# Attention's output rows stored for two tiles at a time, with their buffers first in SBUF

## The chip, the cores and the metric

The kernel runs on one core of one Trainium2 chip. The metric is the device time of one execution in microseconds (us); the time before is the median of three runs.

## The reference

Three layers follow each other. Decayed causal attention without a softmax runs over 8 sequences, 8 heads, 576 positions and 64 features per head. Its result, read as 4608 tokens of 512 features, goes through a mixture of 8 experts in which each token takes only its best expert. The result goes through a third, dense layer with a squared ReLU.

```python
scores = scale * np.matmul(q, k.transpose(0, 1, 3, 2))
ret = scores * Dmat[None, :, :, :]
x = np.matmul(ret, v)            # tokens x 512
...
expert_idx = np.argmax(x @ w_gate, axis=1)
out[mask] = gate_w[mask, None] * (np.maximum(x[mask] @ w1[e], 0.0) @ w2[e])
...
g = np.maximum(x @ w_in, 0.0) ** 2
return g @ w_out
```

## The kernel before

Attention works on 36 tiles of 128 tokens, in a loop over `t` (line 636). Four tiles and a half make one sequence: of every nine tiles, eight belong to one sequence each, four after four, and the ninth holds the last 64 positions of both. `kind(t)` gives a tile's sequence and its place `c` in it (0 to 3, and 4 for the ninth).

A round of the loop does the following, in this order.

- `load(t + 4)` (lines 357 to 364) fetches the inputs of the tile four rounds ahead from `att` in one DMA of 1 MB (768 KB for a ninth tile). There are five buffers of them (`in_p`), so the load waits until the engines have finished with tile t-1.
- In some early rounds small tables are fetched (`tabx`, `idn`, `cf`, `sel`, lines 640 to 651).
- The list `late` of the round before is worked off: four DMAs (line 456) that store the rows of tile t-1, 64 KB each, into the DRAM buffer `x_d`, and for some tiles a store of the logits (`l_d`, line 494).
- In rounds 12, 18, 24 and 30 `load_unit` (line 107) fetches 512 KB of the first experts' weights (`raw`).
- `scores(t + 1)` multiplies keys and queries on TensorE (line 387, `sc`), and VectorE masks them (line 393, `r`).
- `scale_v(t + 2)` scales the values on GpSimd (line 374, `vs`).
- In every second round the transposes of `fold()` (line 476) and the matmuls of `logits()` (line 467) run on TensorE for two tiles at a time.
- `out_x(t)` (lines 420 to 460) sums the tile's output in PSUM (lines 428, 435 and 439). VectorE scales it into `x` (line 447), half of a buffer for two tiles, and transposes it in blocks of 32 into `xr` (line 449), a buffer of 2 KB per partition. There are three such buffers (`xr_p`, one tile each). The round then puts the store of `xr` on the list `late`.
- `state(t)` updates the running state (line 411, `stp`), which ScalarE copies out (line 418, `sts`).
- One step of the routing of a group of finished tiles is taken from the list `todo`.

All these DMAs are issued by the SP queue, in the order of the program. Each of them signals one of eight semaphores (`DMAHW0` to `DMAHW7`), which are used in turn; before an issue the queue waits until the earlier DMA on the same semaphore has landed.

In round 31 `lead_rows` (line 582) fetches the first 256 routed rows from `x_d` with two indirect DMAs of GpSimd (line 270, `lead`); in rounds 33 and 34 TensorE transposes them (line 286, `turn`), and after the loop it starts on the first expert with them. The other rows of the first expert are gathered from `x_d` when the last group is routed (`gather(0, ...)`, `xs<-x_d,gidx`), and their transposed halves go into `xt` (line 782).

The pools of the attention part are opened one behind the other from the left of SBUF: tables, a weight buffer, the five input buffers, `vs`, `r`, and last `xr_p`. When they are closed the pools of the expert stage take the same bytes: `xt_p` first, then `w_b`, then `h_p`, the hidden layer. A new tile waits for what used its bytes before.

Behind attention come the experts (lines 794 to 832) and the dense layer (from line 1106); the change doesn't touch them.

Of the kernel before, what the change touches and what calls it, by code (L numbers as in the profile page):

```python
# [7 lines left out]
F32 = mybir.dt.float32  # L8
# [41 lines left out]
def body(ctx, tc, att, tab_v, tab_x, masks, wg, ident, pick, cst, wu, wd, out):  # L50
# [3 lines left out]
    def scope(stack, name, bufs, space=None, side=None, reuse=None):  # L54
        kw = {"space": space, "side": side, "reuse_waits": reuse}
        kw = {k: v for k, v in kw.items() if v is not None}
        return stack.enter_context(tc.tile_pool(name=name, bufs=bufs, **kw))
# [14 lines left out]
    x_d = dram.tile([NTOK, 512], F32, name="x_d")  # L72
# [253 lines left out]
    lg_ps = scope(chain, "lg_ps", 1, PSUM, side="right")  # L326
    rt_ps = scope(chain, "rt_ps", 1, PSUM, side="right")
    with ExitStack() as es:
        tabs = scope(es, "tabs", 1)
        pools["stg"] = scope(es, "astg", 1)  # L330
        in_p = scope(es, "in_p", 5)
        sp_p = scope(es, "sp_p", 3)
        r_p = scope(es, "r_p", 2)
        xr_p = scope(es, "xr_p", 3)
        sc_ps = scope(es, "sc_ps", 3, PSUM)
        x_ps = scope(es, "x_ps", 2, PSUM)
        st_ps = scope(es, "st_ps", 1, PSUM)
# [6 lines left out]
        zq = tabs.tile([128, 4, 3, 64], F32, name="zq")  # L344
        sts = [tabs.tile([128, 4, 128], F32, name=f"sts{i}") for i in range(4)]

        in_t, vs_t, r_t, st_acc, xp_t = {}, {}, {}, {}, {}
        lead_s = []
        late = []

        def kind(t):
            g, c = divmod(t, 9)
            if c == 8:
                return None, 4
            return 2 * g + c // 4, c % 4
# [42 lines left out]
        def stslot(b, c):  # L398
            return sts[2 + b % 2] if c == 3 else sts[c % 2]
# [20 lines left out]
        def out_x(t):  # L420
            b, c = kind(t)
            q = in_t[t][:, 0].rearrange("p (h n) -> p h n", h=4)
            ps = x_ps.tile([128, 4, 128], F32, tag="x", name="x")
            if c == 4:
                for i in range(2):
                    s = stslot(i, 3)
                    for p in range(4):
                        pe.matmul(
                            ps[:, p], s[:, p], zq[:, p, i:i + 2].rearrange("p a n -> p (a n)"),
                            start=(p == 0 and i == 0), stop=False, skip_group_check=True,  # L430
                        )
            elif c > 0:
                s = stslot(b, c - 1)
                for p in range(4):
                    pe.matmul(ps[:, p], s[:, p], q[:, p], start=(p == 0), stop=False, skip_group_check=True)
            for p in range(4):
                for s in range(2):
                    h = 2 * p + s
                    pe.matmul(
                        ps[64 * s:64 * s + 64, p], vs_t[t][:, 64 * h:64 * h + 64],  # L440
                        r_t[t, s][:, p],
                        start=(c == 0 and p == 0), stop=(p == 3), skip_group_check=True,
                    )
            if t % 2 == 0:
                xp_t[t // 2] = xp_p.tile([128, 4, 256], F32, tag="x", name="x")
            x = xp_t[t // 2][:, :, 128 * (t % 2):128 * (t % 2) + 128]
            vec.tensor_tensor(out=x, in0=ps, in1=tabx[:, c], op=ALU.mult)
            xr = xr_p.tile([128, 4, 4, 32], F32, tag="xr", name="xr")
            vec.transpose(
                out=xr.rearrange("q t k j -> q k t j"), in_=x.rearrange("q k (t i) -> q k t i", i=32)  # L450
            )

            def put():
                rows = x_d[128 * t:128 * t + 128, :].rearrange("(t i) (a c) -> a i t c", i=32, a=4)
                for a in range(4):
                    sp.dma_start(
                        out=rows[a], in_=xr[32 * a:32 * a + 32].rearrange("q t k j -> q t (k j)")
                    )

            late.append(put)  # L460

        def logits(j):
# [173 lines left out]
        for t in range(NT):  # L636
# [3 lines left out]
            if t in (1, 2, 4):  # L640
                c = {1: 2, 2: 3, 4: 4}[t]
# [18 lines left out]
            if fold:  # L660
                fold()
                for g in GROUPS:
                    if g[1] == t - 2:
                        todo += group(*g)
            fold = logits((t - 3) // 2) if t % 2 and t > 2 else None
            out_x(t)
            state(t)
            if t + 1 < NT:
# [82 lines left out]
    with ExitStack() as es:  # L751
# [259 lines left out]
        for u in range(NU):  # L1011
# [4 lines left out]
            if u + 1 in work:  # L1016
                what, j, r = work[u + 1]
# [11 lines left out]
            if u in work:  # L1029
                what, j, r = work[u]  # L1030
# [75 lines left out]
    with ExitStack() as es:  # L1106
# [217 lines left out]
        def tile_of(T, what, a, b):  # L1324
            return first_of[T] + ((7 * a + KEPT.index(b)) // 4 if what == "up" else 14 + 8 * a + b // 2)
# [49 lines left out]
        for m, (T, what, a, b) in enumerate(slots):  # L1375
# [23 lines left out]
            t = tile_of(T, what, a, b)  # L1399
# [85 lines left out]
```

## Time and profile before

| | us |
|---|---|
| median of three runs (1402.28, 1406.72, 1415.77) | 1406.72 |
| profiled execution | 1416.54 |
| its span on the core | 1414.7 |
| TensorE busy in the span | 1359.7 (96%) |
| VectorE, ScalarE, GpSimd busy | 831.8, 547.0, 375.4 |

The profiled execution lasted 1.8 us more than the span of its instructions. A busy share is an average over stages that have different limits; the attention loop is the first eighth of the span. In the views below PE is TensorE, PEld its weight loads, DVE VectorE, ACT ScalarE, POOL GpSimd, and SPq the SP queue that issues DMAs. L456 is line 456 of the kernel before. A share of the DMA engines is the mean over sixteen of them.

### The profile page before, as it was taken

To read this page: it belongs to the slowest core of one execution; us is meant where nothing else is said; L and a number is where in the kernel's file an instruction comes from. 1 tells how busy PE (TensorE), PEld (TensorE's weight loads), DVE (VectorE), ACT (ScalarE), POOL (GpSimd) and SP (SyncE) were. 2 spreads that over 40 slices of the span, in tenths; PEclk is the share of its full clock that TensorE was granted. 3 is DMA by queue.
4 is the path that set the end of the run, shared out by engine and by line. 5 is a ranking of instruction groups with operands and counts; after the bars stand their busy time and mean duration, and the time that the engine had idled before them with its cause. 6 is when DMAs were issued, how large, how long until landed. Compare 5 with 4: busy or idle time off the path is not lost.

```text
span 1414.7 us, 21636 instructions
## 1 busy us (share of the span) xinstructions
PE 1359.7 (96%) x8121; PEld 1161.9 (82%) x8121; DVE 831.8 (59%) x1512; ACT 547.0 (39%) x1064; POOL 375.4 (27%) x408
## 2 busy tenths in 40 slices
PE   8988898999989999899999999999999999999998
PEld 6877787888878889798988888888888888888887
DVE  5666765686967768673785466245742556334422
ACT  1222233453434445342554444244432444234321
POOL 2223345747456474611231013000210003000000
PEclk9999999999999999999999999999999999999999
DMA  9999844666666675656776666567666666665563
GB/s 318 291 287 290 249 137 153 219 217 210 210 197 193 199 246 186 208 173 251 275 272 224 212 233 225 205 208 229 222 234 212 214 207 230 212 234 183 204 212 115
DMA packets 107713, 311.03 MB, mean 220 GB/s; under 512 B 20430, under 2 KB 55758, under 8 KB 85584
## 3 DMA queue, kind: packets, MB, share of 16 engines
q1 hardware_dynamic: 97728, 288.41, 59.9%
q0 software_dynamic: 9872, 21.15, 5.1%
q8 instruction: 66, 1.08, 0.3%
q14 instruction: 47, 0.39, 0.1%
HBM read 257.98 MB, written 52.58 MB: 220 GB/s over the span
## 4 chain that ended last, share of the span: by engine, by line
PE 77%; DMA 10%; issue 6%; POOL 2%; DVE 2%; ACT 1%; another core or an unknown queue 1%; SPq 1%; POOLq 0%; DVEq 0%; ACTq 0%
PE b L1149 23%; PE fa L1223 9%; PE fa L1221 9%; PE fa L1222 9%; DMA in<-att 5%; PE l L808 4%; PE acc L830 4%; PE l L807 4%; PE l L806 4%; PE acc L831 4%; PE acc L832 4%; DMA raw<-wu 1%; POOL xs L270 1%; DMA x_d<-xr 1%
## 5 line engine op out<-in xcount | busy, mean ns | idle before, releaser
L1149 PE MATMUL b<-xt,wq 128*128 128x512 f32 (+1 forms) x1296 | 264.7, 362 | 1.8 <-ACT xt L743 0.7
L1149 PEld LDWEIGHTS b<-xt,wq 128*128 128x128 f32 x1296 | 220.9, 188 | 40.6 <-ACT xt L743 1.1
L1221 PE MATMUL fa<-wq,ch 128*128 128x512 f32 x576 | 224.3, 389 | 0.0
L1223 PE MATMUL fa<-wq,cl 128*128 128x512 f32 x576 | 224.3, 389 | 0.0
L1222 PE MATMUL fa<-wq,ch 128*128 128x512 f32 x576 | 224.3, 389 | 0.0
L1211 DVE TENSOR_TENSOR cl<-g,ch 128x512 fp32r<-128x512 f32 (+1 forms) x160 | 108.9, 689 | 173.7 <-ACT ch L1210 171.2
L734 POOL TENSOR_TENSOR xsum<-yf 128x256 f32<-128x256 f32 x80 | 64.1, 809 | 452.3 <-DVE yf L722 386.9
L270 POOL DMA_INDIRECT xs<-x_d,qidx x140 | 154.9, 1106 | 40.0 <-issue 34.9
L1210 ACT ACTIVATE ch<-g 128x512 fp32r<-128x512 f32 (+1 forms) x160 | 91.5, 584 | 182.4 <-PE fa L1222 181.4
L806 PE MATMUL l<-xt,w 128*128 128x320 f32 (+1 forms) x480 | 150.5, 314 | 6.7 <-issue 5.0
L808 PE MATMUL l<-xt,w 128*128 128x320 f32 (+1 forms) x480 | 150.6, 314 | 5.1 <-issue 5.0
L807 PE MATMUL l<-xt,w 128*128 128x320 f32 (+1 forms) x480 | 150.7, 314 | 4.3 <-issue 4.2
L831 PE MATMUL acc<-w,hh 128*128 128x512 f32 x320 | 128.5, 402 | 3.0 <-issue 3.0
L830 PE MATMUL acc<-w,hh 128*128 128x512 f32 x320 | 129.1, 403 | 2.2 <-issue 1.8
L832 PE MATMUL acc<-w,hl 128*128 128x512 f32 x320 | 127.9, 400 | 2.4 <-issue 2.4
L1223 PEld LDWEIGHTS fa<-wq,cl 128*128 128x128 f32 x576 | 108.1, 188 | 22.5 <-DVE cl L1211 0.2
L1222 PEld LDWEIGHTS fa<-wq,ch 128*128 128x128 f32 x576 | 108.2, 188 | 22.5
L1221 PEld LDWEIGHTS fa<-wq,ch 128*128 128x128 f32 x576 | 108.1, 188 | 22.3
L812 ACT ACTIVATE hh<-l 128x320 fp32r<-128x320 f32 (+2 forms) x128 | 54.6, 436 | 178.4 <-PE l L808 107.3
L1135 ACT ACTIVATE s<-b 128x512 f32<-128x512 f32 (+1 forms) x120 | 66.5, 555 | 104.8 <-PE b L1149 104.6
L813 DVE SCALAR_TENSOR_TENSOR hl<-l,hh 128x320 fp32r<-128x320 f32 (+2 forms) x128 | 59.3, 485 | 79.7 <-ACT hh L812 54.0
L806 PEld LDWEIGHTS l<-xt,w 128*128 128x128 f32 x480 | 90.9, 189 | 9.5 <-issue 4.8
(182 smaller groups left out, 2113.0 us busy)
## 6 DMA issues: line engine op xcount, KB each, us to landing
wq<-ws_d SPq DMA_DIRECT2D x142, 1024.0 KB
raw<-wu SPq DMA_DIRECT2D x62, 512.0 KB
in<-att SPq DMA_DIRECT2D x28, 1024.0 KB
craw<-wd SPq DMA_DIRECT2D x32, 512.0 KB
ws_d<-cw SPq DMA_DIRECT2D x24, 512.0 KB
x_d<-xr SPq DMA_DIRECT2D x144, 64.0 KB
out<-fo SPq DMA_DIRECT2D x32, 256.0 KB
yq<-y_d SPq DMA_DIRECT2D x112, 64.0 KB
```

Of the source, the lines that this page charges most:

```text
L270: pool.indirect_dma_start(out=xs, out_offset=None, in_=src, in_offset=bass.IndirectOffsetOnAxis(ap=index, axis=0),)
L806: pe.matmul(ps, w[:, 0, k], hi[:, k, cs], start=(k == 0), stop=False)
L807: pe.matmul(ps, w[:, 0, k], lo[:, k, cs], start=False, stop=False)
L808: pe.matmul(ps, w[:, 1, k], hi[:, k, cs], start=False, stop=(k == 3))
L830: pe.matmul(acc[i], hh[:, cs], w[:, 0], start=(f == 0), stop=False)
L831: pe.matmul(acc[i], hh[:, cs], w[:, 1], start=False, stop=False)
L832: pe.matmul(acc[i], hl[:, cs], w[:, 0], start=False, stop=(f == 7))
L1149: pe.matmul(ps, w[:, a, c], xc[T][i, b][c], start=(i in (5, 1, 4) and m == 0), stop=(m == 5), skip_group_check=True,)
L1211: vec.tensor_tensor(out=lo[:, o], in0=s, in1=hi[:, o].bitcast(F32), op=ALU.subtract)
L1221: pe.matmul(acc[i], hi[:, cs], w[:, 0], start=(f == 0), stop=False)
L1222: pe.matmul(acc[i], hi[:, cs], w[:, 1], start=False, stop=False)
L1223: pe.matmul(acc[i], lo[:, cs], w[:, 0], start=False, stop=(f == 15))
```

## The change

The transposed rows of two tiles now share one buffer of 4 KB per partition, and there are three of those. The tile with even `t` takes a new one, transposes into its first half and stores nothing; the tile with odd `t` transposes into the second half and puts four stores of 128 KB on the list `late`, each for the rows of both tiles. A row in `x_d` is still written in pieces of 512 bytes. The pool `xr_p` is opened first of attention's pools, so that its 12 KB per partition lie where the tables lay, and all others move up.

```diff
     with ExitStack() as es:
+        xr_p = scope(es, "xr_p", 3)
         tabs = scope(es, "tabs", 1)
...
         r_p = scope(es, "r_p", 2)
-        xr_p = scope(es, "xr_p", 3)
...
-        in_t, vs_t, r_t, st_acc, xp_t = {}, {}, {}, {}, {}
+        in_t, vs_t, r_t, st_acc, xp_t, xr_t = {}, {}, {}, {}, {}, {}
...
-            xr = xr_p.tile([128, 4, 4, 32], F32, tag="xr", name="xr")
+            if t % 2 == 0:
+                xr_t[t // 2] = xr_p.tile([128, 8, 4, 32], F32, tag="xr", name="xr")
+            xr = xr_t[t // 2]
             vec.transpose(
-                out=xr.rearrange("q t k j -> q k t j"), in_=x.rearrange("q k (t i) -> q k t i", i=32)
+                out=xr[:, 4 * (t % 2):4 * (t % 2) + 4].rearrange("q t k j -> q k t j"),
+                in_=x.rearrange("q k (t i) -> q k t i", i=32),
             )
+            if t % 2 == 0:
+                return
 
             def put():
-                rows = x_d[128 * t:128 * t + 128, :].rearrange("(t i) (a c) -> a i t c", i=32, a=4)
+                rows = x_d[128 * t - 128:128 * t + 128, :].rearrange("(t i) (a c) -> a i t c", i=32, a=4)
                 for a in range(4):
                     sp.dma_start(
                         out=rows[a], in_=xr[32 * a:32 * a + 32].rearrange("q t k j -> q t (k j)")
```

The SP queue issues 645 rows instead of 717 (a row is an instruction, and a loop of the expert stage counts once). In rounds 14 to 16 of the attention loop it held, before, a load (`in<-att`) and the four stores of the tile before (`x_d<-xr`) in each round; the names in brackets are what each waits for, the DMA semaphores and the engines:

```order
L364 DMA in<-att 128x2048 [waits DMAHW1_49,PE_49,Pool_49]
L456 DMA x_d<-xr 32x4x128 [waits DMAHW2_49,DVE_49]
L456 DMA x_d<-xr 32x4x128 [waits DMAHW3_49]
L456 DMA x_d<-xr 32x4x128 [waits DMAHW4_49]
L456 DMA x_d<-xr 32x4x128 [waits DMAHW5_49]
L364 DMA in<-att 128x2048 [waits DMAHW6_49,PE_49,Pool_49]
L456 DMA x_d<-xr 32x4x128 [waits DMAHW7_49,DVE_49]
L456 DMA x_d<-xr 32x4x128 [waits DMAHW0_49]
L456 DMA x_d<-xr 32x4x128 [waits DMAHW1_49]
L456 DMA x_d<-xr 32x4x128 [waits DMAHW2_49]
L364 DMA in<-att 128x2048 [waits DMAHW3_49,PE_49,Pool_49]
```

The third store of the second round waits for semaphore 1, which is that of the first load above. On the same queue in the same rounds, 14 to 16, the changed kernel has:

```order
L364 DMA in<-att 128x2048 [waits DMAHW5_49,PE_49,Pool_49]
L461 DMA x_d<-xr 32x8x128 [waits DMAHW6_49,DVE_49]
L461 DMA x_d<-xr 32x8x128 [waits DMAHW7_49]
L461 DMA x_d<-xr 32x8x128 [waits DMAHW0_49]
L461 DMA x_d<-xr 32x8x128 [waits DMAHW1_49]
L364 DMA in<-att 128x2048 [waits DMAHW2_49,PE_49,Pool_49]
L364 DMA in<-att 128x2048 [waits DMAHW3_49,PE_49,Pool_49]
L461 DMA x_d<-xr 32x8x128 [waits DMAHW4_49,DVE_49]
L461 DMA x_d<-xr 32x8x128 [waits DMAHW5_49]
L461 DMA x_d<-xr 32x8x128 [waits DMAHW6_49]
L461 DMA x_d<-xr 32x8x128 [waits DMAHW7_49]
```

Two loads now follow each other, and the stores of two tiles come in one block behind them. The second store of round 16 waits for semaphore 5, that of the load of round 14, and the first for semaphore 4, that of the load of round 13.

At the start of the loop, in rounds 1 and 2, the SP queue held before the load of tile 5, a table, the four stores of tile 0, and then the load of tile 6:

```order
L364 DMA in<-att 128x2048 [waits DMAHW7_49,PE_49,Pool_49]
L642 DMA tabx<-tab_x 128x512 [waits DMAHW0_49]
L456 DMA x_d<-xr 32x4x128 [waits DMAHW1_49,DVE_49]
L456 DMA x_d<-xr 32x4x128 [waits DMAHW2_49]
L456 DMA x_d<-xr 32x4x128 [waits DMAHW3_49]
L456 DMA x_d<-xr 32x4x128 [waits DMAHW4_49]
L364 DMA in<-att 128x2048 [waits DMAHW5_49,PE_49,Pool_49]
L642 DMA tabx<-tab_x 128x512 [waits DMAHW6_49]
L646 DMA idn<-ident 128x128 [waits DMAHW7_49]
```

The same rounds of the changed kernel's SP queue:

```order
L364 DMA in<-att 128x2048 [waits DMAHW7_49,PE_49,Pool_49]
L647 DMA tabx<-tab_x 128x512 [waits DMAHW0_49]
L364 DMA in<-att 128x2048 [waits DMAHW1_49,PE_49,Pool_49]
L647 DMA tabx<-tab_x 128x512 [waits DMAHW2_49]
L651 DMA idn<-ident 128x128 [waits DMAHW3_49]
L461 DMA x_d<-xr 32x8x128 [waits DMAHW4_49,DVE_49]
L461 DMA x_d<-xr 32x8x128 [waits DMAHW5_49]
L461 DMA x_d<-xr 32x8x128 [waits DMAHW6_49]
L461 DMA x_d<-xr 32x8x128 [waits DMAHW7_49]
```

The load of tile 6 and two tables moved ahead of the first stores, which are now those of tiles 0 and 1. On the other engines the instructions stand as before.

## Rows read from the trace of the kernel before

**Rows 1.** The page: TensorE and DMA in 40 slices; packets by size.
```profile
PE   8988898999989999899999999999999999999998
...
DMA  9999844666666675656776666567666666665563
...
DMA packets 107713, 311.03 MB, mean 220 GB/s; under 512 B 20430, under 2 KB 55758, under 8 KB 85584
```

**Rows 2.** Chain of waits, 84 to 110 us: start, length, what.
```profile
79.74 8.90 DMA x_d<-xr
...
88.71 8.17 DMA in<-att
...
98.11 8.06 DMA in<-att
...
108.61 8.71 DMA in<-att
```

**Rows 3.** Timeline of the SP queue, 93 to 112.4 us: start, issue time, what.
```profile
93.28 0.58 SPq L364 DMA_DIRECT2D in<-att  x1
...
98.11 0.39 SPq L364 DMA_DIRECT2D in<-att  x1
...
101.50 0.30 SPq L456 DMA_DIRECT2D x_d<-xr  x1
...
101.84 0.43 SPq L456 DMA_DIRECT2D x_d<-xr  x1
102.32 0.57 SPq L107 DMA_DIRECT2D raw<-wu  x1
103.00 0.58 SPq L364 DMA_DIRECT2D in<-att  x1
...
106.19 0.33 SPq L456 DMA_DIRECT2D x_d<-xr  x1
...
112.08 0.31 SPq L456 DMA_DIRECT2D x_d<-xr  x1
```

**Rows 4.** Waits of the SP queue, 45 to 160 us.
```profile
SPq L456 <- DMA in<-att: 38.3, 25, 2.6
```

**Rows 5.** Instructions on the input tiles, 45 to 160 us: durations, first and last start.
```profile
L364 SPq DMA_DIRECT2D in<-att x24: 351/471/1576, 46.4 to 155.3; - x24
```

**Rows 6.** Busy time by stretch; the last two columns are DMA share and GB/s.
```profile
10.00:25.00 15.00, 13.55 (x194) 11.95 (x194) 6.79 (x11) 2.65 (x7) 4.92 (x5) 0.94 1.03 392
25.00:30.00 5.00, 3.10 (x44) 2.37 (x40) 3.22 (x6) 0.76 (x2) 1.34 (x2) 0.90 0.78 215
45.00:160.00 115.00, 98.17 (x1461) 84.03 (x1459) 77.43 (x165) 26.57 (x65) 32.86 (x28) 0.99 0.93 289
176.00:179.30 3.30, 3.30 (x37) 3.01 (x36) 3.13 (x10) 0.00 (x0) 0.00 (x0) 1.00 0.37 89
```

**Rows 7.** Waits of VectorE, 45 to 160 us.
```profile
DVE xr L449 <- DMA x_d<-xr: 24.7, 20, 2.8
DVE x L447 <- PE x L439: 12.5, 11, 2.4
```

**Rows 8.** Timeline of the SP queue, 13 to 22 us.
```profile
14.01 5.11 SPq L456 DMA_DIRECT2D x_d<-xr  x4
21.60 0.35 SPq L364 DMA_DIRECT2D in<-att  x1
```

**Rows 9.** Chain of waits, 158 to 172 us, and TensorE's timeline there.
```profile
161.50 6.96 DMA lead<-x_d,lead_idx
...
168.51 0.66 PE L286 MATMUL turn<-idn,lead 128*128 128x128 f32 x4 [0.47 <-DMA lead<-x_d,lead_idx]
```

**Rows 10.** Timelines of the SP queue and of GpSimd behind the loop.
```profile
180.02 1.77 SPq L456 DMA_DIRECT2D x_d<-xr  x4
...
189.34 1.00 POOL L270 DMA_INDIRECT xs<-x_d,gidx  x1 [18.87 <-DVE g L266]
```

**Rows 11.** Chain of waits, 119.1 to 131.5 us.
```profile
123.23 1.09 PE sc L387 x16
...
130.84 0.49 PE stp L411 x16
```

## Prediction

> **What bounds the kernel now.** I read the page's forty slices first [rows 1]. TensorE is at 8 tenths or more in every slice, so over the whole span it is the bound; the DMA engines stand at 9 tenths in the first four slices alone, about 140 us, and those are the attention loop that the change touches. There the next view is the chain of work [rows 2]: from 88.71 to 117.3 us it is almost only loads of attention's inputs, 8.06 to 8.71 us each, with short pieces of the SP queue between them. TensorE shows up on the chain for longer runs only later. The stage is therefore bound by its loads, and what the change is worth is read from what a load waits for.
>
> The SP queue tells that [rows 3]. Each DMA on it signals one of eight semaphores in turn, and waits first until the DMA that used the same one eight places earlier has landed (both listings of the change show the waits). A tile now has one load and four stores, so the third store of a tile always waits for the load issued at the start of the round before. In [rows 3] the load issued at 93.28 us lands and lets a third store go at 101.50, and the one of 98.11 does so at 106.19; the next load stands behind that store. In the stretch from 45 to 160 us this wait is 38.3 us in 25 times [rows 4], one for each tile. So two loads are in flight at most, and one for the moment between a landing and the next issue. Two rounds last one load and what stands behind its landing: in [rows 2] the load of 88.71 lands after 8.17 us, and the next but one is issued at 98.11, 9.40 us later, or 4.70 per tile. The loop's own count agrees: 24 issues from 46.4 to 155.3 us [rows 5], 108.9 / 23 = 4.74 us per tile.
>
> Is a load's 8 us latency, or are the DMA engines full? [rows 6] has three stretches. While almost only loads run (10 to 25 us) they move 392 GB/s at a share of 1.03. While stores alone run (176 to 179.3) 89 GB/s take a share of 0.37: 1.22 us of the sixteen engines for 294 KB. In the mixed stretch they are at 0.93, but with only 289 GB/s. A tile's load, 1.05 MB at 392 GB/s, is 2.68 us; its stores, 262 KB at 1.22 us for 294 KB, are 1.09; the 23 rounds, 7 to 29, also hold three weight loads of 0.52 MB (rounds 12, 18 and 24), which add 3 x 1.34 / 23 = 0.17. That makes 3.94 of the 4.74 us. The remaining 0.80 us per tile is lost: 0.33 as idle engines (0.07 x 4.74), and 0.47 as packets that last longer than in either pure stretch. It isn't a tax on every byte: between the landings at 106.19 and 112.08 [rows 3] one more load of 0.52 MB was fetched (issued at 102.32, directly before another load), and that interval, 5.89 us, is only 1.20 longer than the 4.69 before it, at 437 GB/s for the added bytes. A load behind a load is cheap; what costs is the change from stores to a load, one per tile.
>
> **The change part by part.** Stores: 144 of 64 KB become 72 of 128 KB. The bytes and the rows of 512 bytes stay, so the 1.09 us of the engines per tile stay. The queue's order becomes load, four stores, load, load, four stores: one change from stores to a load in two tiles instead of two. If the lost 0.80 us belongs to these changes, half of it goes: 0.40 us per tile. Its ends: nothing, if it belongs to bytes that are mixed; and 0.47 / 2 + 0.33 = 0.57, if the idle part goes as well. I take 0.40, since the row of 112.08 puts it on the change of direction, and since some idleness is bound to stay. It counts for the loads of tiles 6 to 35: 30 x 0.40 = 12.0 us, with ends 0 and 17.
>
> Semaphores: with six DMAs for two tiles, the waits that fall on loads are now on the first two stores of a pair. The load of tile t+3 stands behind the landing of tile t's, three stores and itself (about 1.9 us by the issue times in [rows 3]); three rounds must hold 8.17 + 1.9 us, so this queue no longer binds above 3.4 us per tile. SP's own time falls as well; it is no bound either way.
>
> The transposes: the buffer of a tile is now free when its store of three tiles before has landed. In 45 to 160 us VectorE waits 24.7 us for that, 20 times [rows 7]. A store can take 8.90 us to land [rows 2]. Three buffers of two tiles each give four rounds between a pair's issue and the next write into its buffer, some 17 us, so this wait goes. I count nothing for it: VectorE's next wait in [rows 7] is TensorE, and TensorE's in this stage is the load. Were that cover gone, it is inside the 0.80 us.
>
> The start: the load of tile 6 is issued at 21.60 us, after the first tile's four stores, which take SP from 14.01 to 19.1 [rows 8]; now it stands ahead of them. The engines have a share of 0.78 from 25 to 30 us [rows 6], so at most 1.1 us is gained, and none is lost; I take 1.0.
>
> What is late next: the first routed rows are fetched at 161.50 us and reach TensorE 6.96 us later, two rounds after their indices [rows 9]; TensorE then waits 0.47 us for them. Two rounds shorter by 0.80 us together leave 0.8 us uncovered: I take 0.8 off, ends 0 and 2. At the end the last stores go out together with those of the tile before, 256 KB more, 1.1 us at the rate above. The gather that needs them starts at 189.34 us [rows 10], 7.5 us after the last store's issue at about 181.8, and it waits for VectorE's indices: nothing, and at most 1.1 if that cover were gone.
>
> The pool's place: the row buffers lie under the two buffers that the first expert's columns take, where before they lay under the hidden layer's last ones. Those columns are written after the gather, which needs all stores anyway; nothing, and at most the same 1.1 us.
>
> Sum: 12.0 + 1.0 - 0.8 = 12.2 us. The profiled execution took 1416.54 us (span 1414.7, 1.8 around it), 0.7% over the median of the runs shown, 1406.72; it becomes 1404.3 us, and the median 1394.5.
>
> Here the Trainium skill speaks against the change. Its page "DMA: Bandwidth & Descriptors", section "Why small descriptors are slow", puts the price of small transfers on the single descriptor (a fixed overhead in each, and metadata for each), and a store's rows remain 512 bytes on both sides. By that rule alone the stores would cost what they cost, and the gain would be nothing, the second rival below. The page of the profile agrees that most packets are small: 55758 of 107713 are under 2 KB [rows 1]; but 437 GB/s for a load behind a load is not in that rule, and so it doesn't decide.
>
> **The rivals.** TensorE's own pace: from 123.23 to 131.33 us the chain is TensorE without a gap [rows 11], two tiles in 8.10 us, 4.05 per tile. If the whole lost time goes, the loop falls to this floor: 30 x (4.74 - 4.05) = 20.7 us, 1386.0. For it: the sum of the pure rates, 3.94 us, is below the floor. Against: with two bounds this close, each waits for the other at times.
>
> Nothing happens: the lost 0.80 us goes with stores beside loads, however they are grouped, and the loop stays at 4.74. The time is 1406 give or take 3. For it: the bytes, rows and buffers of loads are unchanged. Against: the 437 GB/s.
>
> Slower: in the SP queue two loads now stand behind four stores whose first two wait for the two loads before, so loads are issued in bursts. This decides when three rounds of 4.74 us no longer hold a load and the 1.9 us behind it: from 12.3 us of a load's latency. To be 14.1 us slower, 1%, it takes 0.47 us more per tile, a latency of 13.7; that gives 1421. Latency is 8.06 to 8.71 us, and a burst of stores twice as long adds 1.09, so there is room. If transposes still waited for stores, the change wouldn't do what it says: by [rows 7] and 8.90 us to land against 17 there is no case for it.
>
> **How the numbers follow.** One per cent, 14.1 us, is about what a measurement of this kernel tells from no change. The forecast, 1394.5 us, has a chance of 0.55, with a range of its own from 1388 to 1401; some 45% of it lies below 1392.6. TensorE's floor has 0.19, nothing 0.18, slower 0.08. Faster by over 1%: 0.55 x 0.45 + 0.19 = 0.44. Slower by over 1%: 0.08. Within 1%: 0.48. The range reaches from a little under the floor to the case of nothing: 1384 to 1407.
>
> **What would show it.** Right: the x_d stores appear 72 times; the wait of the transposes for them is gone; loads in the stretch come every 4.2 to 4.4 us with a DMA rate above 305 GB/s; the first transposed tile of the first expert comes 10 to 14 us earlier, and everything behind is shifted by as much. Wrong: still 4.7 us per tile with the transposes free (then the lost time belongs to mixed bytes), a pace of 4.05 with TensorE gapless (then the switch cost all of it), load latencies over 12 us (then the bursts), or a gain in the loop that is gone by the end.

## The result and the profile after

The changed kernel takes 1386.05 us in the median of five runs (1383.41 to 1394.09). Its time is 0.9858 of the time before, with a 95% interval from 0.9808 to 0.9907: 20.0 us less, 13.1 to 27.0. The profiled execution took 1389.07 us with a span of 1387.3. It is 27.5 us shorter than the profiled one of before, which lay 9.8 us over its median while this one lies 3.0 over its own; the medians differ by 20.7. Ratios are formed from undisturbed runs alone, so they can differ a little from the quotient of two medians.

The page first, against [rows 1]: TensorE, DMA engines and packets.

```profile
PE   8999998998999989999999999999999999999998
...
DMA  9999644566757656665866676656666766565563
...
DMA packets 106560, 311.02 MB, mean 224 GB/s; under 512 B 19278, under 2 KB 54606, under 8 KB 84432
```

1153 packets are gone, and TensorE's row has a 9 in four of its first five slices, where it had one. The stretches that answer to [rows 6], with the engines' columns first and the clock, DMA share and GB/s last:

```profile
25.00:30.00 5.00, 4.31 (x72) 3.65 (x68) 4.47 (x8) 1.17 (x4) 1.04 (x1) 1.00 1.06 390
45.00:160.00 115.00, 113.57 (x1687) 97.97 (x1686) 96.12 (x200) 31.38 (x75) 38.22 (x31) 1.00 0.92 308
45.00:140.00 95.00, 93.99 (x1432) 81.22 (x1431) 80.39 (x162) 25.09 (x61) 31.62 (x26) 1.00 1.01 346
```

From 45 to 160 us TensorE is busy for 113.57 us instead of 98.17. The third row ends soon after the last load's issue at 136.3 us: 346 GB/s, where [rows 6] had 289. The attention loop is now bound by TensorE, as the chain of waits says for 84 to 112 us (start, length, what), where [rows 2] had loads of 8 us:

```profile
85.12 1.09 PE sc L387 x16
...
89.68 1.09 PE sc L387 x16
...
95.22 1.23 DVE a L227
...
99.77 1.60 DVE b L240
...
101.86 1.31 PE sc L387 x16
...
106.32 1.09 PE sc L387 x16
...
110.16 1.09 PE sc L387 x16
```

Between these stand other matmuls and, from 93.10 to 101.42 us, a piece of VectorE's work (routing, masks, scaling and transposes); no load. The waits of the SP queue, 45 to 160 us, against [rows 4]:

```profile
SPq L364 <- PE stp L411: 26.2, 11, 4.4
SPq L461 <- DVE xr L451: 13.4, 8, 5.7
```

The 38.3 us of waiting for loads to land are gone, all but 1.1: the loads now wait until TensorE has finished with a buffer, and the stores until VectorE has written the rows. The loads themselves (against [rows 5]):

```profile
L364 SPq DMA_DIRECT2D in<-att x23: 328/454/2131, 45.4 to 136.3; - x23
```

That is 90.9 / 22 = 4.13 us per load instead of 4.74. A loop's pace is better read from what it produces. The transposes between 45 and 145 us, first in the kernel before:

```profile
L449 DVE STREAM_TRANSPOSE xr<-x x21: 711/711/714, 45.9 to 141.5; 128x512 f32<-128x512 f32 x21
```

and after:

```profile
L451 DVE STREAM_TRANSPOSE xr<-x x25: 711/711/714, 47.0 to 142.6; 128x512 f32<-128x512 f32 x25
```

95.6 us held 20 tiles before and 24 after, 4.78 and 3.98 us per tile. VectorE waits for no store any more; what is left against [rows 7] is TensorE:

```profile
DVE x L447 <- PE x L439: 13.8, 14, 2.3
```

Behind the loop (timelines of GpSimd and TensorE, against [rows 9, 10]), the first expert's gather starts at 167.50 us instead of 189.34, 21.8 us earlier, and the transposes of the lead rows start with no wait in front:

```profile
140.50 1.19 POOL L270 DMA_INDIRECT lead<-x_d,lead_idx  x1 [3.52 <-DVE lead_idx L592]
...
167.50 1.00 POOL L270 DMA_INDIRECT xs<-x_d,gidx  x1 [18.79 <-DMA raw<-wu]
```
```profile
146.81 0.66 PE L286 MATMUL turn<-idn,lead 128*128 128x128 f32 x4
```

### The profile page after: what moved, and what is told of

Same layout as the page of the kernel before. It is cut to its first block, busy times and chain, and to the rows that moved or that the text cites. A ratio compares the mean times of both kernels' runs of the same rounds, so it can differ in the third digit from the quotient of the medians.

```text
span 1387.3 us, 21515 instructions
## 1 busy us (share of the span) xinstructions
PE 1352.8 (98%) x8121; PEld 1159.2 (84%) x8121; DVE 835.3 (60%) x1512; ACT 547.3 (39%) x1064; POOL 377.3 (27%) x408
## 3 DMA queue, kind: packets, MB, share of 16 engines
q8 instruction: 66, 1.08, 0.3%
## 4 chain that ended last, share of the span: by engine, by line
PE 83%; issue 6%; DMA 4%; DVE 3%; POOL 2%; ACT 1%; another core or an unknown queue 1%; SPq 0%; DVEq 0%; POOLq 0%; ACTq 0%
PE b L1154 24%; PE fa L1227 9%; PE fa L1228 9%; PE fa L1226 9%; PE l L811 4%; PE l L813 4%; PE l L812 4%; PE acc L835 4%; PE acc L836 4%; PE acc L837 3%; PE sc L387 2%; PE x L439 2%; PE x L435 1%; POOL xs L270 1%
```

## The experiments

Four theories were open, of which the prediction held the first. **A**: each change from stores to a load costs, and there are half as many. **B**: the transposes no longer wait for stores. **C**: with fewer DMAs per tile the eight semaphores come round more slowly, so more loads are in flight. **D**: the place of the pool matters.

### e1: the buffers alone

```diff
+        xr_p = scope(es, "xr_p", 6)
...
-        xr_p = scope(es, "xr_p", 3)
```

This is the kernel before, with six buffers of one tile and the pool first.

> The kernel before with six buffers for the transposed rows of one tile each (pool first) instead of three: the transposes no longer wait for stores, while loads and stores keep their order, sizes and number. If the changes from stores to a load are what cost (theory A), or the eight semaphores (theory C): the loop stays at 4.6 to 4.8 us per tile and the time within 4 us of before. If the gain came from freeing the transposes (theory B): 4.0 us per tile and about 20 us less than before, as in the changed kernel.

Measured: 1408.3 us (1396.66 to 1420.16), 0.9972 of before [0.9933, 1.001]. Its SP queue waits, 45 to 160 us, and its transposes over the whole program:

```profile
SPq L456 <- DMA in<-att: 38.9, 24, 2.5
```
```profile
L449 DVE STREAM_TRANSPOSE xr<-x x36: 711/711/714, 11.5 to 177.7; 128x512 f32<-128x512 f32 x36
```

Its profiled execution, 1420.16 us, is the longest of its ten runs, so only its loop is read here. The transposes have no wait for stores, and yet the loop from the first to the last lasts 166.2 us; in the kernel before it is 166.1:

```profile
L449 DVE STREAM_TRANSPOSE xr<-x x36: 710/711/714, 13.2 to 179.3; 128x512 f32<-128x512 f32 x36
```

The queue's wait for loads is what it was. B falls, and so does the pool's place as a gain by itself.

### e2: two pair stores in every round

```diff
-                for a in range(4):
...
+                def some(these):
+                    for a in these:
...
+                some((0, 1))
+                late.append(lambda: some((2, 3)))
```

The changed kernel, with the same 72 stores of 128 KB, but two of them in each round: load, two stores, load, two stores. There is a change from stores to a load in every tile again.

> The changed kernel with the four 128 KB stores of a pair issued two in the even and two in the odd round: as few DMAs and semaphores, the same buffers, but again one change from stores to a load in each tile. Theory A: most of the gain is lost, 4.4 to 4.7 us per tile and 12 to 20 us more than the changed kernel. Theories B (transposes) and C (semaphores): as the changed kernel, 4.0 us per tile, within 4 us of it.

Measured: 1387.36 us (1383.05 to 1389.78), 0.9859 [0.981, 0.9909]: as the changed kernel.

```profile
L451 DVE STREAM_TRANSPOSE xr<-x x36: 711/711/714, 13.1 to 157.0; 128x512 f32<-128x512 f32 x36
```

The loop lasts 143.9 us; that of the changed kernel, 11.5 to 157.4, lasts 145.9. A change of direction in every tile costs this loop nothing, and A falls. A price that TensorE's pace could hide is looked for in m3 below.

### e3: pairs in eight stores of 64 KB

```diff
-                for a in range(4):
+                for h in range(2):
+                    for a in range(4):
```

The changed kernel with the grouping of two loads and one block of stores, but each store halved.

> The changed kernel with each pair stored in eight DMAs of 64 KB at once instead of four of 128 KB: changes from stores to a load as in the changed kernel, but ten DMAs for two tiles on the eight semaphores, as before. Theory A alone: 4.0 to 4.2 us per tile, within 6 us of the changed kernel. Theory C: the eighth store waits for the load issued just ahead of the block, so that at most two loads are in flight: 4.5 us per tile or more, 12 to 25 us more than the changed kernel. Theory B: as the changed kernel.

Measured: 1418.41 us (1411.77 to 1426.15), 1.0078 [1.0047, 1.0108], slower than before. The SP queue's waits, 45 to 140 us, and the transposes:

```profile
SPq L462 <- DMA in<-att: 31.2, 18, 3.1
```
```profile
L451 DVE STREAM_TRANSPOSE xr<-x x36: 711/711/715, 11.6 to 183.7; 128x512 f32<-128x512 f32 x36
```

With ten DMAs for two tiles the seventh and eighth store take the semaphores of the two loads directly ahead of the block. The queue stands until these have landed, and only then come the next loads. The loop lasts 172.1 us, and the time is 32.4 us over the changed kernel's, more than the 12 to 25 expected for C. This speaks for C, but a fixed price for each DMA of 64 KB would do the same; the next six kernels take that apart.

### m1 to m4: the transfers alone

These kernels compute nothing of the reference. They only move attention's bytes: 36 loads of 1 MB into five buffers, and 9.4 MB of stores. For every one or two tiles the loop issues (written short):

```diff
-        load(t); store(t, 1)                                           # m1
+        load(t); load(t + 1); store(t, 2)                              # m2
+        load(t); store(t, 2, (0, 1)); load(t + 1); store(t, 2, (2, 3)) # m3
+        load(t) for all t; then store(t, 2) for all pairs              # m4
```

`store(t, 1)` is four stores of 64 KB, `store(t, 2)` four of 128 KB for two tiles, and with two numbers in brackets only two of these.

> Attention's DMAs alone, without any computation: 36 loads of 1 MB into five buffers and 144 stores of 64 KB, in the order of before (one load, four stores). Theory A, with pure rates of 2.68 us for a load and 1.09 for a tile's stores and about 0.8 us for a change from stores to a load: 4.5 us per tile, 155 to 170 us. If a change of direction costs nothing: 3.8 us per tile, 135 to 140 us.

> The same bytes in the order of the changed kernel: two loads, four stores of 128 KB. Theory A: half the changes, 4.1 us per tile, 10 to 20 us less than with one load and four stores. If the cost belongs to mixed bytes or there is none: the same time as that run within 4 us.

> The same 128 KB stores, but two behind each load. Theory A: as with one load and four stores of 64 KB, 4.4 us per tile or more, although there are as few DMAs as in the order of pairs. If the number of DMAs is what counts (theory C): as the order of pairs.

> All 36 loads first, then all 72 stores of 128 KB: one change of direction. Every theory: the sum of the pure rates, 36 x 3.77 = 136 us or a little less, 2.6 to 2.7 us for a load and 1.0 to 1.1 for a tile's stores. It gives the floor against which the other three orders are held.

Measured, one execution each: m1 172.72 us, m2 123.94, m3 125.96, m4 131.43. Two met neither of their numbers: m1 is slower than both, and m2 is 48.8 us below it, where A had 10 to 20. So m1 has the pace of the loop before, 4.6 to 4.75 us per tile, with no engine computing at all. m3 changes direction in every tile and takes 2.0 us more than m2, 0.11 us for each of 18 further changes if they are all of it, while m4, with one change in all, is slower than both. A falls a second time. The loads of m1 in 20 to 100 us, and how long one takes from issue to landing:

```profile
L48 SPq DMA_DIRECT2D in<-att x17: 430/569/767, 23.2 to 96.6; - x17
...
DMA to landing us min/median/max: 7.8/8.1/8.6
```

and of m3:

```profile
L48 SPq DMA_DIRECT2D in<-att x24: 398/428/471, 22.7 to 97.1; - x24
...
DMA to landing us min/median/max: 9.1/9.2/9.8
```

In m3 a load takes longer to land, 9.2 instead of 8.1 us, and yet they come every 3.23 us (74.4 / 23) instead of 4.59 (73.4 / 16): three are in flight instead of two. With five DMAs per tile the third store waits for the load of the round before, and one more store and the next load stand behind it, so two rounds hold a load's time to land and these three issues: (8.1 + 2 x 0.45 + 0.57) / 2 = 4.8 us per tile, with 0.45 us for a store's issue and 0.57 for a load's. With three DMAs per tile the second store waits for the load of two rounds before, and three rounds hold the sum: (9.2 + 0.4 + 0.43) / 3 = 3.3. Measured are 4.59 and 3.23.

### m5 and m6: loads in flight, or the number of DMAs

m5 is m3 with two buffers for the loads, so that a load waits for the last but one to land; its stores keep their 128 KB. m6 is m1 with the loads issued by GpSimd, on semaphores of their own.

```diff
 m5:
-    in_p = ctx.enter_context(tc.tile_pool(name="in_p", bufs=5))
+    in_p = ctx.enter_context(tc.tile_pool(name="in_p", bufs=2))
 m6:
-        sp.dma_start(out=a, in_=att[t])
+        nc.gpsimd.dma_start(out=a, in_=att[t])
```

> Attention's transfers alone again, nothing else is computed: one load of 1 MB and two stores of 128 KB for each tile, in the order of m3 (1 load, 2 stores, 1 load, 2 stores), the same number of DMAs and the same bytes as m3, but with two buffers for the loads in place of five, so that the load of tile t+2 starts only after the load of tile t has landed. If the loads in flight decide (theory C as it stands: eight semaphores taken in turn leave two loads in flight where a tile has five DMAs), this falls from m3's 3.4 us per tile to the pace of m1 although every store has 128 KB: 165 to 175 us in all. If it is the number of DMAs that costs (a fixed price for each DMA of 64 KB, about 0.6 us each by m1 against m3: 46.8 us over 72 DMAs), it stays at 124 to 130 us. In between, both have a share.

> Attention's transfers alone, nothing else is computed: loads of 1 MB and four stores of 64 KB for each tile as in m1, the same number of DMAs as m1, but the loads are issued by GpSimd, whose queue has semaphores of its own, so that five loads are in flight (five buffers are written in turn) and the stores on SyncE no longer hold them back. If the loads in flight decide (C), 64 KB stores cost little by themselves: 120 to 140 us. If each DMA of 64 KB has a fixed price of 0.6 us, 160 to 175 us as m1.

Measured, one execution each: m5 151.9 us, in between its two numbers; m6 153.44, which met neither. Both ran on another chip, on which the kernel before takes 1373.52 us instead of 1405.21; the DMA rate of the changed kernel from 10 to 25 us is 407 GB/s there (e5) and 405 in the result's trace. m5's row for 20 to 100 us (the last columns are the clock, DMA share and GB/s), and its loads:

```profile
20.00:100.00 80.00, 0.00 (x0) 0.00 (x0) 1.00 0.99 328
```
```profile
L48 SPq DMA_DIRECT2D in<-att x21: 357/358/358, 19.8 to 99.3; - x21
...
DMA to landing us min/median/max: 7.3/7.9/8.4
```

Two in flight instead of three, with nothing else changed in the program, cost 25.9 of the 46.8 us that lie between m3 and m1. The other 20.8 us, 0.58 per tile, are not the loads' number. By the formula above they are what stands between a landing and the next load: in m1 two stores and a longer issue, (2 x 0.45 + 0.57 - 0.36) / 2 = 0.55. The rows bear this out: two rounds take 2 x 4.59 = 9.18 us in m1 and 2 x 3.98 = 7.95 in m5 (79.5 / 20); less a load's 8.1 and 7.9 us to land, 1.08 and 0.05 us are left between a landing and the load behind it. So of the 0.61 us per tile between the two paces 0.51 are the queue's issues, and 0.10 are loads that take longer to land. What 64 KB stores cost on a queue that holds no load back was not run by itself.

At 3.98 us per tile the transfers of m5 already keep the pace of the changed kernel's loop, with two loads in flight and no store between a landing and the next load. Whether the kernel needs the third load in flight, or only fewer stores behind a landing, is therefore open; fewer DMAs per tile give both.

m6 was meant to show it, and does not. Its five loads in flight filled the engines, 419 GB/s from 20 to 100 us, but the stores beside them took 21.2 us to land in the median and fell behind; then they ran alone, at 133 GB/s and a DMA share of 0.55 from 105 to 145 us. Two things changed at once there, the loads in flight and the queue they share the engines with, and no verdict on the price of a 64 KB store follows.

For comparison m2 and m3 in the same stretch:

```profile
20.00:100.00 80.00, 0.00 (x0) 0.00 (x0) 1.00 1.04 405
20.00:100.00 80.00, 0.00 (x0) 0.00 (x0) 1.00 1.05 408
```

### e4 to e6: the pool's place

The changed kernel, with the pool where it stood before:

```diff
-        xr_p = scope(es, "xr_p", 3)
         tabs = scope(es, "tabs", 1)
...
         r_p = scope(es, "r_p", 2)
+        xr_p = scope(es, "xr_p", 3)
```

> The changed kernel with the pool of the row buffers laid out last again, as before. The hidden layer's buffers then lie over it, and the last of them wait for the last stores. If the place is worth nothing: the changed kernel's time within 3 us. If it carries part of the gain: 3 to 10 us more, in the first expert's matmuls behind the loop and not in the loop.

Measured in e4: 1398.22 us (1385.33 to 1404.59, nine runs), 0.9937 [0.9894, 0.998]. The runs lay too far apart to tell scatter from the place, so it was run again (e6) beside the changed kernel itself (e5).

> The changed kernel itself, on the same chip and beside the same runs of the kernel before as e6, so that the place of the pool (theory D) can be read from the two directly. If the place is worth nothing, both have the same time within 3 us, near 1386 or wherever this chip puts them; if the place is worth what the first run of the pool laid out last hinted (1398.22 against 1386.05), this one is 9 to 15 us faster than e6.

> The change without its second half: pair stores, but the pool of the rows laid out where it stood before. The first time this kernel had 1398.22 in the median with runs from 1385.33 to 1404.59, while its profiled run had the shortest span but one (1383.5). If the place of the pool costs nothing and the first result was scatter, it agrees with e5 within 3 us; if the place matters (D), it is 9 to 15 us slower than e5 and the ratio to the kernel before is near 0.994 again.

Measured, on a chip on which the kernel before takes 1373.52 us: e5 1354.04 (0.9853 [0.9836, 0.987]), e6 1359.98 (0.9903 [0.989, 0.9917]). The intervals don't overlap; the place is worth 5.9 us beside the pairs, less than the 9 to 15 that the first run hinted at. The timeline of VectorE in e6 behind the loop, with the wait in brackets, and TensorE's stretches there (busy, clock, DMA share, GB/s):

```profile
158.32 0.71 DVE L451 STREAM_TRANSPOSE xr<-x 128x512 f32<-128x512 f32 x1
163.51 0.42 DVE L818 SCALAR_TENSOR_TENSOR hl<-l,hh 128x256 fp32r<-128x256 f32 x1 [4.48 <-DMA x_d<-xr]
```
```profile
160.00:165.00 5.00, 1.17 (x11) 0.85 0.85 220
165.00:170.00 5.00, 5.00 (x21) 0.50 0.35 102
170.00:175.00 5.00, 5.00 (x41) 0.97 0.54 210
```

The same two views of e5:

```profile
159.67 0.71 DVE L451 STREAM_TRANSPOSE xr<-x 128x512 f32<-128x512 f32 x1
160.31 0.38 DVE L818 SCALAR_TENSOR_TENSOR hl<-l,hh 128x256 fp32r<-128x256 f32 x1
```
```profile
160.00:165.00 5.00, 5.00 (x43) 1.00 0.73 140
165.00:170.00 5.00, 5.00 (x41) 1.00 1.02 323
```

`hl` is the first expert's hidden layer for the lead rows. With the pool last VectorE waits 4.48 us for the stores of the last pairs to land before it writes `hl`; `hl` comes to lie where their rows are. TensorE is idle for 3.83 of the 5 us, and then its clock is granted at 0.50, the lower of its two levels, for the next 5 us, half of which is lost: 3.83 + 2.5 = 6.3 us by the rows, 5.9 by the times. e4 has the same wait, 4.4 us. In the trace of the kernel before `hl` waits for no store, so the pairs bring the wait about, and the pool's place takes it away again. On this chip the change gains 19.5 us, and with the pool last 13.5 of them remain.

## Why the prediction was right, and where not

It said 1394.5 us, 12.2 less than before; measured is 20.0 less [13.1 to 27.0]. The direction and the stage were right, and the time is in the range of 1384 to 1407. But it lies below the forecast's own range, 1388 to 1401, and 12.2 us is outside the interval. What came out is the rival with TensorE's own pace, 1386.0, to which the prediction gave 0.19. That it agrees to a tenth of a microsecond is luck: the interval is 13.9 us wide, and the rival's sum leaves the start out.

**What bounds the loop.** Right: loads, two in flight because the third store waits on the semaphore of the load before (the second one in a round with a weight load, as at 106.19 us). m1 has that pace with no compute at all.

**The lost 0.80 us per tile.** This is the step that failed. The prediction laid pure rates end to end (3.94 us), called the rest lost, and put it on "the change from stores to a load, one per tile", of which half would go: 0.40 us. It had the right account one paragraph before: a load's 8.17 us and what stands behind its landing, shared by two loads in flight, which alone is 4.70. There was nothing else to explain; idle engines and longer packets are what two loads in flight look like. e2 keeps a change of direction in every tile and loses nothing by it, and m3 loses 0.11 us per change at most. The interval at 437 GB/s, on which the step rested, held one transfer more between two landings: it showed that one more in flight is cheap, not that a change of direction is dear.

**Semaphores.** Right, and treated as a side remark: "this queue no longer binds above 3.4 us per tile". m3 comes to 3.23 and m2 to 405 GB/s, so 3.4 was nearly the price of the transfers without compute. Had the 0.80 us been tied to it, the loop would have come out at the next bound, TensorE's: 4.05 in the rival, 3.98 in the trace. From the first transpose to the last the loop lost 166.1 - 145.9 = 20.2 us, 1.5 of them up to tile 6 and 18.7 behind it, where the sum had 12.0.

**The transposes' wait.** Right: gone, and worth nothing by itself (e1).

**The start.** About right: from the first transpose to that of tile 6 it takes 26.4 us (11.49 to 37.87) instead of 27.9 (13.18 to 41.10), 1.5 less against the forecast 1.0; in e2, whose first rounds fetch the same, 25.1.

**What is late next.** The 0.8 us for late lead rows did not come: `turn` starts with no wait. The rows are fetched at 140.50 us, and TensorE is busy with the loop until it takes them at 146.81, 6.3 us later; before, they were fetched 7.0 us ahead and TensorE waited 0.47. The gather behind the last stores starts 21.8 us earlier. That is the loop's whole 20.2 and the 1.7 us by which the first transpose came earlier in this trace; the changed kernel doesn't always have these 1.7, since e2's first transpose comes at 13.1.

**The pool's place.** "Nothing, and at most the same 1.1 us" was right for the sum and wrong as a reading. It looked at what the new place collides with, and not at what the larger buffers would collide with in the old one. There 4.48 us of waiting and a lower clock, 5.9 us in all, would have been lost (e6).

**The rule on small descriptors.** The Trainium skill's page "DMA: Bandwidth & Descriptors", section "Why small descriptors are slow", taken alone, would have left the time as it was. The rows of 512 bytes stayed, and 20 us went; m2 moves the same rows beside loads at 405 GB/s. In this case the queue decided: how many loads were in flight, and what stood behind a landing.

**The rival on the slower side.** Loads in bursts did not hurt here. What does is e3: the same bursts with eight stores, where the semaphores come round within one round. That point lay between four and eight stores per pair, and the prediction looked for it in a load's latency instead.

## What to carry to other kernels

Where a queue's DMAs take a few semaphores in turn, count the DMAs between two loads: that number says, as far as the buffers go, how many loads are in flight, and the pace is a load's time to land plus what stands behind the landing, divided by the loads in flight. Merge the small transfers until the next engine is the bound, and look which DMA each semaphore wait falls on before changing the order. When a buffer grows, see also which later tile takes its bytes, since that tile's first write waits for the buffer's last transfer.

## What the runs showed of the hardware

A share of busy DMA engines near 1 does not mean that they are full: m5 has 0.99 at 328 GB/s, m3 1.05 at 408 with the same packets. With two loads in flight instead of three the engines count as busy 17% longer for the same bytes ((0.99 / 328) / (1.05 / 408)).

Stores beside loads cost less than alone. In m4, first with loads alone and then with stores alone:

```profile
20.00:80.00 60.00, 0.00 (x0) 0.00 (x0) 1.00 1.01 422
100.00:125.00 25.00, 0.00 (x0) 0.00 (x0) 1.00 0.99 247
```

A load alone takes 2.49 us (25 issues from 20.5 to 80.2 us) and a tile's stores alone 1.06 (262 KB at 247 GB/s), together 3.55; mixed, in m3, a tile takes 3.23.

The Trainium skill's page "DMA: Bandwidth & Descriptors", section "Specifications", gives about 358 GB/s as the limit of one core at HBM, half of what two cores share. m2 moves 405 GB/s in both directions together, and m4's loads alone 422 from 20 to 80 us, so the measurement decides here.
